# A residual quantizer on one core: the order of all instructions planned by forward and backward passes in place of one pass by due times

## The chip, the cores and the metric

The kernel runs on one core of a Trainium2 chip. The metric is the time on the device in microseconds. The kernel before has three runs, the median is 826.91 us (818.86 to 829.97).

## The reference

```python
# x: (2, 16000, 512) bf16; dw_enc, dw_dec: (3, 512); codebooks: (4, 8, 512)
z = sum(xp[:, i:i+T, :] * dw_enc[i] for i in range(3))      # depthwise, three taps in time
res = z = silu(z)
q = 0
for s in range(4):                                          # residual quantization
    cb = codebooks[s]
    d2 = |res|^2 - 2 res.cb^T + |cb|^2                      # (B, T, 8)
    sel = cb[d2.argmin(-1)]
    q, res = q + sel, res - sel
y = sum(qp[:, i:i+T, :] * dw_dec[i] for i in range(3))      # three taps again
```

For every one of 32000 time steps the input is filtered, passed through SiLU, and replaced by four code words of eight each; each word is picked for what the words before it left over. The output is a filter over the sums of the words.

## The kernel before, in words

The 32000 rows are spread as 128 partitions of 250 rows ("groups"), and the groups are worked off in 16 chunks of 12, then 14 times 16, then 14 groups (`SIZES`). A chunk passes through these tasks:

- *Load.* One transposing DMA for each group and its two neighbours (L358, queue of SP) brings the channels onto the partitions, into XT (two buffers). The first chunk is loaded plainly and transposed on the PE.
- *Front.* For each of four blocks of 128 channels: three products by a tap (L410, DVE), two sums (L418, DVE), then SiLU as exp (L422, ACT), one added (L426, DVE), log (L430, ACT), exp (L433, ACT) and the product (L438, DVE) into RES.
- *Four stages.* `score`: for five or six groups at a time the PE multiplies RES by itself and by the code words into a bank of psG (L489, L494; two banks); `norm` (L502) and `dots` (L505) read it out on DVE. Six small DVE steps (L522 to L549) make a one-hot code; the PE turns it (L559), ACT copies it (L566). Then the chosen words are taken off RES in eight-row pieces: either the PE picks the words (SEL, L584, two banks of psD) and DVE subtracts (L596), or the PE adds RES and the words (NEW, L601 and L584, psA) and ACT writes the sum back (L607). `ON_DVE` says how many of the four blocks go to DVE.
- *Output.* From the turned one-hot codes of the last stage the PE makes the filtered sums of words (Y, L633, psA), ACT copies them out (L639, three buffers YSB), SP's queue stores them (L643).

The order of the instructions on every engine is made in Python while the kernel is built. `Plan.add` takes a task with its engine, the time that it holds the engine (`hold`), the time until its result is there (`delay`), what it needs, and a due time; `take` and `give` name buffers. `Plan.run` plays the tasks through once, with a clock of its own: whenever an engine is free it takes the ready task with the earliest due time for which a buffer is free, and emits its instructions at once. Due times come from the chunk's place (`org`), the period (56) and the stage. Where the PE has nothing to do and was busy for less than 60% of the last 4 planned microseconds (`WARM`), a matmul that fills time goes in (L313). Loads, stores and the steps of the first chunk's load are planned as engines of their own (SP, OUT, ROWS), though loads and stores share SP's queue. The chip's engines each run their instructions in the order emitted and wait for each other by semaphores; the planned times themselves are not in the program.

Of the kernel before, what the change touches and what calls it, by code (L numbers as in the profile page):

```python
# [2 lines left out]

# [14 lines left out]
GC = 16  # L19
# [11 lines left out]
WARM = 0.6  # L31
# [4 lines left out]
PERIOD, LEAD, STAGE, LATE, SPREAD = 56, 0.4, 0.9, 0.3, 0.3  # L36
FAR = -3.3e38


class Plan:  # L40

    def __init__(self, slots):
        self.slots = dict(slots)
# [4 lines left out]
        self.tasks.append((engine, hold, delay, [n for n in needs if n is not None], due, emit, take, give))  # L50
        return len(self.tasks) - 1

    def run(self):
        tasks = self.tasks
        left = [len(t[3]) for t in tasks]
        after = [[] for _ in tasks]
        for n, t in enumerate(tasks):
            for d in t[3]:
                after[d].append(n)
        engines = list(dict.fromkeys(t[0] for t in tasks))  # L60
        ready = {e: [] for e in engines}
        until = {e: 0.0 for e in engines}
        spans = []
        for n, t in enumerate(tasks):
            if not left[n]:
                heapq.heappush(ready[t[0]], (t[4], n))
        now, events, order = 0.0, [], []
        while len(order) < len(tasks):
            going = True
            while going:  # L70
                going = False
                for e in engines:
                    if until[e] > now + 1e-9:
                        continue
                    passed, pick = [], None
                    while ready[e]:
                        due, n = heapq.heappop(ready[e])
                        if all(self.slots[k] > 0 for k in tasks[n][6]):
                            pick = n
                            break  # L80
                        passed.append((due, n))
                    for p in passed:
                        heapq.heappush(ready[e], p)
                    if pick is None:
                        if e == "PE" and self.idle and self.slots["psG"] > 0:
                            while spans and spans[0][1] < now - 4.0:
                                spans.pop(0)
                            if sum(b - max(a, now - 4.0) for a, b in spans) < 4.0 * WARM and self.idle():
                                until[e] = now + 0.3
                                spans.append((now, until[e]))  # L90
                                heapq.heappush(events, (until[e], -1))
                        continue
                    _, hold, delay, _, _, emit, take, _ = tasks[pick]
                    for k in take:
                        self.slots[k] -= 1
                    order.append(pick)
                    emit()
                    until[e] = now + hold
                    if e == "PE":
                        spans.append((now, until[e]))  # L100
                    heapq.heappush(events, (now + hold, -1))
                    heapq.heappush(events, (now + max(hold, delay), pick))
                    going = True
            if len(order) == len(tasks):
                break
            now = events[0][0]
            while events and events[0][0] <= now + 1e-9:
                _, n = heapq.heappop(events)
                if n < 0:
                    continue  # L110
                for k in tasks[n][7]:
                    self.slots[k] += 1
                for a in after[n]:
                    left[a] -= 1
                    if not left[a]:
                        heapq.heappush(ready[tasks[a][0]], (tasks[a][4], a))


@with_exitstack
def kernel(  # L120
# [227 lines left out]
    def load(st, org):  # L348
        g0, G, GP = st["g0"], st["G"], st["GP"]
        done = []  # L350
        if g0 == 0:
            load_rows(st, org)
            return

        def one(n):
            if n == 0:
                st["XT"] = xpool.tile([P, KT, GC + 2, P], BF16, name="XT")
            nc.sync.dma_start_transpose(out=st["XT"][:, :, n, :], in_=group_rows(g0 + n - 1))  # L358

        def edge(n):  # L360
            st["XE"] = const.tile([P, KT, P], BF16, name="XE")
            nc.sync.dma_start_transpose(out=st["XE"], in_=group_rows(0))

        def shift(n):
            XT, XE = st["XT"], st["XE"]
            nc.gpsimd.tensor_copy(XT[:, :, n, 0:P - 1], XE[:, :, 1:P])
            for b in range(B):
                p = (b + 1) * HB - 1
                nc.gpsimd.memset(XT[:, :, n, p:p + 1], 0.0)
            if GP > G:  # L370
                nc.gpsimd.memset(XT[:, :, G + 2:GP + 2, :], 0.0)

        for n in range(G + 2):
            due = org - 2.2 * PERIOD + 0.01 * n
            inside = 0 <= g0 + n - 1 < S
            t = plan.add("SP", 1.4, 2.2, done[-1:], due, (lambda n=n: one(n)) if inside else (lambda n=n: edge(n)),
                         take=("XT",) if n == 0 else ())
            done.append(t)
            if not inside:
                st["edge"] = plan.add("POOL", 1.0, 1.4, [t], due, lambda n=n: shift(n))  # L380
        st["loaded"] = [done[-1], st.get("edge")]

    def front(st, org):
        n, G, MB = st["n"], st["GP"], st["MB"]
# [18 lines left out]
        def block(i):  # L403
# [44 lines left out]
            hold, delay = dve(0.67), dve(0.67) + 0.1  # L448
            z = plan.add("DVE", hold, delay, st["loaded"], due, lambda: product(0), take=("Z",))
            t = plan.add("DVE", hold, delay, st["loaded"], due, lambda: product(1), take=("T",))  # L450
            z = add_up(1, [z, t])
            t = plan.add("DVE", hold, delay, st["loaded"], due, lambda: product(2), take=("T",), give=("XT",) if i == KT - 1 else ())
            st["taps"].append(t)
            z = add_up(2, [z, t])
            e = plan.add("ACT", act(1.8), act(1.8) + 0.12, [z], due, exp, take=("E",))
# [13 lines left out]
    def stage(st, s, due):  # L469
# [11 lines left out]

        def score(q, m):
            RES = st["RES"]
            if q == 0:
                u["TR"] = small.tile([P, GC], BF16, name="TR")
                u["PR"] = small.tile([P, GC, C], BF16, name="PR")
            PS = pending.pop() if pending else psG.tile([P, 512], F32, name="PS")
            V = u["V", q] = PS[:, 0:m * (hi - lo)].rearrange("p (r c) -> p r c", r=m)
            nc.tensor.matmul(V[:, :, own:own + HT], lhsT=IDENT, rhs=MASK[:, 0:m, :], start=True, stop=False, skip_group_check=True)  # L489
            for r in range(m):  # L490
                for i in range(KT):
                    for h in range(2):
                        half = RES[:, i, 2 * (q + r) + h, :]
                        nc.tensor.matmul(V[h * HT:(h + 1) * HT, r, :], lhsT=half[:, LC:LC + HT], rhs=half[:, lo:hi],  # L494
                                         start=False, stop=(i == KT - 1), skip_group_check=True)
            if s == Nq - 1 and q + m == G:
                free["RES"].append(RES)
            if not scored[2:]:
                scored.append(None)
# [9 lines left out]
        for n in range(banks):  # L509
            m = -(-(G - q) // (banks - n))  # L510
            needs = [st["new"][i, j] for i in range(KT) for j in range(q // MB, (q + m - 1) // MB + 1)]
            needs += scored[0:2] + ([codes[st["n"]]] if st["n"] < 3 else [])
            t = plan.add("PE", 0.05 + 0.25 * m, 0.25 + 0.25 * m, needs, due, lambda q=q, m=m: score(q, m), take=("psG",),
                         give=("RES",) if s == Nq - 1 and q + m == G else ())
            seen.append(t)
            maxima.append(plan.add("DVE", 0.07 + 0.065 * m, 0.2 + 0.065 * m, [t], due, lambda q=q, m=m: norm(q, m)))
            maxima.append(plan.add("DVE", 0.06 + 0.01 * m, 0.2, [maxima[-1]], due, lambda q=q, m=m: dots(q, m), give=("psG",)))
            q += m
# [91 lines left out]
        for j in range(0, J, 2):  # L610
            for i in range(KT):
                if i < on_dve[s]:
                    for k in (j, j + 1):
                        c = plan.add("PE", 0.25 * f, 0.25 * f + 0.2, [t, words], due, lambda i=i, k=k: chosen(i, k), take=("psD",))
                        st["new"][i, k] = plan.add("DVE", 0.1 + 0.53 * f, 0.2 + 0.53 * f, [c] + seen, due,
                                                   lambda i=i, k=k: subtract(i, k), give=("psD",))
                    continue
                c = plan.add("PE", 0.86 * f, 0.86 * f + 0.2, [t, words, st["new"][i, j], st["new"][i, j + 1]], due,
                             lambda i=i, j=j: rest(i, j), take=("psA",))
                st["new"][i, j] = st["new"][i, j + 1] = plan.add("ACT", 0.13 + 0.8 * f, 0.25 + 0.8 * f, [c] + seen, due,  # L620
                                                                 lambda i=i, j=j: keep(i, j), give=("psA",))
# [112 lines left out]
```

## Time and profile before

| | before |
|---|---|
| time of the runs, median (lowest to highest) | 826.91 us (818.86 to 829.97) |
| profiled execution, span (its own time is told by the span alone) | 824.6 us |
| PE, matmul | 653.2 us busy, 79% |
| PE, weight load | 314.0 us, 38% |
| DVE | 752.2 us, 91% |
| ACT | 717.8 us, 87% |
| mean granted clock of the PE | 0.912 |
| DMA | 71.82 MB, mean 87 GB/s |

The span runs from the first to the last instruction of one execution. Busy time is time in which an engine executes; an engine that waits for a semaphore is idle. Two instructions of an engine can overlap, so a step from start to start can be shorter than the duration shown. A release ("<- PE SEL L584") names what ended an idle time.

### The profile page before, as it was taken

Reading aid. Unit: us, or ns where it says so; the run is one execution under the profiler, and the core shown is the slowest. Engines: PE = TensorE matmul, PEld = TensorE weight load, DVE = VectorE, ACT = ScalarE, POOL = GpSimd, SP = SyncE. Lnnn points to the kernel's source line nnn. Section 1 sums busy time; section 2 is a strip of 40 time slices with the busy share of each in tenths; the row PEclk is TensorE's granted clock in tenths of the full one; section 3 lists DMA queues with packets and bytes.
Section 4 is the critical chain, followed back from the end, with each engine's and each line's share of the span. In section 5 each row is a group of like instructions: output and inputs, shape, how many; then the busy total and the mean of one; then the engine's idle time right before and its main releaser. Section 6 shows DMA issues by size and latency. Waiting matters only on the chain.

```text
span 824.6 us, 23407 instructions
## 1 busy us (share of the span) xinstructions
PE 653.2 (79%) x10289; PEld 314.0 (38%) x10289; DVE 752.2 (91%) x1584; ACT 717.8 (87%) x623; POOL 7.4 (1%) x17
## 2 busy tenths in 40 slices
PE   3047697898788879868888788779898888989995
PEld 2023333443343444424444244334434434334442
DVE  5987999999999999999999999998989999988871
ACT  2659788898999999999999999998989999886564
POOL 1100000000000000000000000000000000000000
PEclk9566877798998999999999999998979999989998
DMA  7442422152452635253716353451615301111132
GB/s 172 48 98 61 86 52 59 34 117 39 109 111 53 136 70 99 59 119 72 160 53 148 59 117 72 89 138 42 135 44 110 98 36 70 52 79 52 79 143 114
DMA packets 156207, 71.82 MB, mean 87 GB/s; under 512 B 147401, under 2 KB 147786, under 8 KB 155978
## 3 DMA queue, kind: packets, MB, share of 16 engines
q1 hardware_dynamic: 155152, 69.64, 35.8%
q8 instruction: 80, 1.31, 0.7%
q0 software_dynamic: 672, 0.43, 0.5%
q10 hardware_dynamic: 282, 0.26, 0.1%
q14 instruction: 21, 0.17, 0.1%
HBM read 2.39 MB, written 32.77 MB: 43 GB/s over the span
## 4 chain that ended last, share of the span: by engine, by line
ACT 41%; DVE 31%; PE 22%; issue 3%; DMA 2%; ACTq 0%; DVEq 0%
ACT RES L607 11%; ACT LN L430 8%; ACT YSB L639 7%; ACT E L422 7%; ACT E L433 7%; DVE Z L418 6%; DVE RES L596 6%; PE PS L494 6%; PE NEW L601 5%; DVE TR L502 4%; DVE RES L438 3%; DVE T L410 3%; PE NEW L584 3%; PE Y L633 3%; PE SEL L584 2%
## 5 line engine op out<-in xcount | busy, mean ns | idle before, releaser
L607 ACT ACTIVATE RES<-NEW 128x1024 bf16<-128x1024 f32 (+1 forms) x238 | 234.7, 1037 | 29.2 <-PE NEW L584 24.6
L494 PE MATMUL PS<-RES 128*64 128x80 bf16 (+1 forms) x8064 | 189.3, 208 | 27.4 <-DVE RES L438 26.7
L596 DVE TENSOR_TENSOR RES<-RES,SEL 128x512 bf16<-128x512 bf16 (+1 forms) x292 | 185.7, 674 | 19.6 <-PE SEL L584 19.2
L494 PEld LDWEIGHTS <-RES 128*64 128x64 bf16 x8064 | 165.6, 119 | 75.5 <-issue 36.8
L601 PE MATMUL NEW<-RES,IDENT 128*128 128x512 bf16 (+1 forms) x476 | 154.2, 408 | 30.8 <-ACT RES L607 27.0
L418 DVE TENSOR_TENSOR Z<-Z,T 128x2048 bf16<-128x2048 bf16 (+1 forms) x128 | 153.7, 1200 | 0.0
L639 ACT ACTIVATE YSB<-Y 128x1024 bf16<-128x1024 f32 (+1 forms) x126 | 128.1, 1042 | 17.8 <-PE Y L633 12.0
L422 ACT ACTIVATE E<-Z 128x2048 bf16<-128x2048 bf16 (+1 forms) x64 | 122.6, 1916 | 16.2 <-DVE Z L418 16.2
L430 ACT ACTIVATE LN<-E 128x2048 f32<-128x2048 bf16 (+1 forms) x64 | 122.3, 1913 | 8.0 <-DVE E L426 8.0
L433 ACT ACTIVATE E<-LN 128x2048 bf16<-128x2048 f32 (+1 forms) x64 | 122.8, 1920 | 0.2
L502 DVE TENSOR_REDUCE TR<-PS 128x5 bf16<-128x320 f32 (+1 forms) x188 | 95.5, 510 | 17.9 <-PE PS L494 17.5
L633 PE MATMUL Y<-A,OHT 128*128 128x512 bf16 x249 | 86.4, 390 | 30.5 <-ACT RES L607 17.2
L584 PE MATMUL SEL<-OHT,CBN 32*128 32x512 bf16 (+1 forms) x292 | 84.4, 397 | 27.3 <-ACT OHT L566 15.5
L584 PE MATMUL NEW<-OHT,CBN 32*128 32x512 bf16 (+1 forms) x476 | 97.8, 407 | 0.0
L410 DVE TENSOR_SCALAR T<-XT,WENC 128x2048 bf16<-128x2048 bf16 (+1 forms) x128 | 93.5, 740 | 0.0
L584 PEld LDWEIGHTS <-CBN 32*128 32x128 bf16 x768 | 35.2, 92 | 149.9 <-issue 144.4
L438 DVE TENSOR_TENSOR RES<-Z,E 128x2048 bf16<-128x2048 bf16 (+1 forms) x64 | 76.9, 1202 | 6.6 <-ACT E L433 4.0
L601 PEld LDWEIGHTS <-IDENT 128*128 128x128 bf16 x476 | 33.7, 99 | 106.0 <-issue 103.8
L489 PE MATMUL PS<-MASK,IDENT 128*128 128x320 bf16 (+1 forms) x188 | 62.6, 333 | 10.4 <-DVE PR L505 10.1
L633 PEld LDWEIGHTS <-OHT 128*128 128x128 bf16 x373 | 32.5, 98 | 70.2 <-issue 46.9
L566 ACT ACTIVATE OHT<-ps_oh 128x512 bf16<-128x512 bf16 (+1 forms) x64 | 39.7, 623 | 17.0 <-PE ps_oh L559 16.9
L633 PE MATMUL Y<-B,OHT 128*128 128x512 bf16 x124 | 47.4, 383 | 0.1
(73 smaller groups left out, 370.9 us busy)
## 6 DMA issues: line engine op xcount, KB each, us to landing
out_dram<-YSB SPq DMA_DIRECT2D x61, 512.0 KB, 3.2
XT<-in_x_dram SPq DMA_TRANSPOSE x267, 2.8
RES<-in_x_dram SPq DMA_DIRECT2D x1, 1664.0 KB, 6.9
out_dram<-YSB SPq DMA_DIRECT2D x1, 384.0 KB, 2.3
out_dram<-YSB SPq DMA_DIRECT2D x1, 256.0 KB
A<-in_dw_dec_dram POOLq DMA_DIRECT2D x2, 96.0 KB, 5.3
CB<-in_codebooks_dram ACTq DMA_DIRECT2D x1, 128.0 KB
A<-in_dw_dec_dram POOLq DMA_DIRECT2D x2, 64.0 KB, 4.8
```

The lines of the kernel that those rows point to most:

```text
L418: nc.vector.tensor_tensor(out=z, in0=z, in1=t, op=ALU.add)
L422: nc.scalar.activation(u["E"][:, 0:G, :], u["Z"][:, 0:G, :], ACT.Exp, scale=-1.0)
L430: nc.scalar.activation(u["LN"][:, 0:G, :], u["E"][:, 0:G, :], ACT.Ln)
L433: nc.scalar.activation(u["E"][:, 0:G, :], u["LN"][:, 0:G, :], ACT.Exp, scale=-1.0)
L494: nc.tensor.matmul(V[h * HT:(h + 1) * HT, r, :], lhsT=half[:, LC:LC + HT], rhs=half[:, lo:hi], start=False, stop=(i == KT - 1), skip_group ...
L502: nc.vector.tensor_reduce(out=u["TR"][:, q:q + m], in_=u["V", q][:, :, own:own + HT], axis=AX.X, op=ALU.max)
L584: nc.tensor.matmul(ps, lhsT=CBN[s][rows, i * P:(i + 1) * P], rhs=u["OHT"][rows, 0:MB, :], start=start, stop=True, skip_group_check=True)
L596: nc.vector.tensor_tensor(out=old, in0=old, in1=u["SEL", i, j][:, 0:W].rearrange("p (m t) -> p m t", t=HT), op=ALU.add)
L601: nc.tensor.matmul(NEW[:, h, 0:W], lhsT=IDENT, rhs=tokens(i, j + h, 1), start=True, stop=False, skip_group_check=True)
L607: nc.scalar.activation(old, u["NEW", i, j][:, :, 0:W].rearrange("p h (m t) -> p h m t", t=HT), ACT.Copy)
L633: nc.tensor.matmul(Y[:, h, :], lhsT=lhs(), rhs=rhs, start=(a == 0), stop=(a == len(terms) - 1))
L639: nc.scalar.activation(u["YSB"][:, k:k + n, :], u[k][:, 0:n, :], ACT.Copy)
```

## The change

The change rewrites how `Plan.run` finds the order. The plan is played forward with ranks in place of due times, then backward (from the end, with needs and buffers reversed), ranked by when each task ended in the forward pass, then forward again by the backward times, and so on. There are three rounds, each of which begins with ranks disturbed at random from a fixed seed. The last forward pass gives the order and the planned starts; `emit` then hands out the instructions in that order and puts in the matmuls that fill time by the same rule as before (fewer in number: 51 in place of 100).

```diff
+ROUNDS = [(2428, 1.0, 9), (1053, 1.0, 7), (1916, 0.3, 6)]
...
-    def run(self):
+    def pass_over(self, rank, backward=False):
+
         tasks = self.tasks
-        left = [len(t[3]) for t in tasks]
+        needs = [t[3] for t in tasks]
...
+        if backward:
+            needs, after = after, needs
+        takes, gives = (7, 6) if backward else (6, 7)
...
-                        due, n = heapq.heappop(ready[e])
-                        if all(self.slots[k] > 0 for k in tasks[n][6]):
+                        at, n = heapq.heappop(ready[e])
+                        if all(slots[k] > 0 for k in tasks[n][takes]):
...
+    def run(self):
+
+        tasks = self.tasks
+        last = [max(t[1], t[2]) for t in tasks]
+        rank = [t[4] for t in tasks]
+        for seed, spread, passes in ROUNDS:
+            rng = random.Random(seed)
+            starts, order = self.pass_over([r + rng.gauss(0.0, spread) for r in rank])
+            for _ in range(passes):
+                ends, _ = self.pass_over([-(a + d) for a, d in zip(starts, last)], backward=True)
+                starts, order = self.pass_over([-(a + d) for a, d in zip(ends, last)])
+            rank = starts
+        self.emit(starts, order)
```

Beside that, planned times are corrected, and what the order may do is loosened or pinned down in a few places:

```diff
+        room = plan.add("SP", 0.0, 0.0, [], org - 2.2 * PERIOD, place, take=("XT",))
         for n in range(G + 2):
...
-            t = plan.add("SP", 1.4, 2.2, done[-1:], due, (lambda n=n: one(n)) if inside else (lambda n=n: edge(n)),
-                         take=("XT",) if n == 0 else ())
+            t = plan.add("SP", 1.31, 2.9, [room], due, (lambda n=n: one(n)) if inside else (lambda n=n: edge(n)))
...
-        st["loaded"] = [done[-1], st.get("edge")]
+        st["loaded"] = done + [st.get("edge")]
...
-            t = plan.add("DVE", hold, delay, st["loaded"], due, lambda: product(2), take=("T",), give=("XT",) if i == KT - 1 else ())
+            t = plan.add("DVE", hold, delay, st["loaded"] + (st["taps"] if i == KT - 1 else []), due, lambda: product(2), take=("T",), give=("XT",) if i == KT - 1 else ())
...
-            if q == 0:
+            if "TR" not in u:
...
+            if s == Nq - 1 and q + m == G:
+                needs += seen
...
-            t = plan.add("PE", 0.05 + 0.25 * m, 0.25 + 0.25 * m, needs, due, lambda q=q, m=m: score(q, m), take=("psG",),
+            t = plan.add("PE", 0.05 + 0.21 * m, 0.25 + 0.21 * m, needs, due, lambda q=q, m=m: score(q, m), take=("psG",),
...
-                        c = plan.add("PE", 0.25 * f, 0.25 * f + 0.2, [t, words], due, lambda i=i, k=k: chosen(i, k), take=("psD",))
+                        c = plan.add("PE", 0.3 * f, 0.3 * f + 0.2, [t, words], due, lambda i=i, k=k: chosen(i, k), take=("psD",))
...
-                c = plan.add("PE", 0.86 * f, 0.86 * f + 0.2, [t, words, st["new"][i, j], st["new"][i, j + 1]], due,
+                c = plan.add("PE", 0.92 * f, 0.92 * f + 0.2, [t, words, st["new"][i, j], st["new"][i, j + 1]], due,
```

The transposes of a chunk no longer wait for each other in the plan, only for room in XT. The instructions themselves, their sizes and the split between the engines are as before.

More of the change, by code (lines that the diff above doesn't have):

```diff
@@ L2 @@
 import heapq
+import random
 from contextlib import ExitStack
@@ L51, in add @@
         return len(self.tasks) - 1
-    def run(self):
+    def pass_over(self, rank, backward=False):
         tasks = self.tasks
-        left = [len(t[3]) for t in tasks]
+        needs = [t[3] for t in tasks]
         after = [[] for _ in tasks]
-        for n, t in enumerate(tasks):
-            for d in t[3]:
+        for n, ds in enumerate(needs):
+            for d in ds:
                 after[d].append(n)
+        if backward:
+            needs, after = after, needs
+        takes, gives = (7, 6) if backward else (6, 7)
+        left = [len(d) for d in needs]
         engines = list(dict.fromkeys(t[0] for t in tasks))
@@ L62, in run @@
         until = {e: 0.0 for e in engines}
-        spans = []
+        slots = dict(self.slots)
         for n, t in enumerate(tasks):
             if not left[n]:
-                heapq.heappush(ready[t[0]], (t[4], n))
-        now, events, order = 0.0, [], []
-        while len(order) < len(tasks):
+                heapq.heappush(ready[t[0]], (rank[n], n))
+        now, events, order, starts = 0.0, [], [], [0.0] * len(tasks)
+        while True:
             going = True
@@ L76, in run @@
                     while ready[e]:
-                        due, n = heapq.heappop(ready[e])
-                        if all(self.slots[k] > 0 for k in tasks[n][6]):
+                        at, n = heapq.heappop(ready[e])
+                        if all(slots[k] > 0 for k in tasks[n][takes]):
                             pick = n
                             break
-                        passed.append((due, n))
+                        passed.append((at, n))
                     for p in passed:
@@ L84, in run @@
                     if pick is None:
[L85 to L91, printed above, removed]
                         continue
-                    _, hold, delay, _, _, emit, take, _ = tasks[pick]
-                    for k in take:
-                        self.slots[k] -= 1
+                    t = tasks[pick]
+                    for k in t[takes]:
+                        slots[k] -= 1
                     order.append(pick)
[L97 to L102, printed above, removed]
+                    starts[pick] = now
+                    until[e] = now + t[1]
+                    heapq.heappush(events, (now + t[1], -1))
+                    heapq.heappush(events, (now + max(t[1], t[2]), pick))
                     going = True
             if len(order) == len(tasks):
-                break
+                return starts, order
             now = events[0][0]
@@ L110, in run @@
                     continue
-                for k in tasks[n][7]:
-                    self.slots[k] += 1
+                for k in tasks[n][gives]:
+                    slots[k] += 1
                 for a in after[n]:
@@ L115, in run, with emit @@
                     if not left[a]:
-                        heapq.heappush(ready[tasks[a][0]], (tasks[a][4], a))
+                        heapq.heappush(ready[tasks[a][0]], (rank[a], a))
+    def run(self):
[10 more added lines that the diff above has]
+        self.emit(starts, order)
+    def emit(self, starts, order):
+        tasks = self.tasks
+        free, back, spans, end = self.slots["psG"], [], [], 0.0
+        for n in order:
+            engine, hold, delay, _, _, emit, take, give = tasks[n]
+            at = starts[n]
+            if engine == "PE":
+                while end + 0.3 <= at:
+                    while back and back[0] <= end:
+                        free += 1
+                        heapq.heappop(back)
+                    while spans and spans[0][1] < end - 4.0:
+                        spans.pop(0)
+                    if free > 0 and sum(b - max(a, end - 4.0) for a, b in spans) < 4.0 * WARM and self.idle():
+                        spans.append((end, end + 0.3))
+                        end += 0.3
+                    else:
+                        end += 0.1
+                while back and back[0] <= at:
+                    free += 1
+                    heapq.heappop(back)
+                end = at + hold
+                spans.append((at, end))
+            free -= take.count("psG")
+            for _ in range(give.count("psG")):
+                heapq.heappush(back, at + max(hold, delay))
+            emit()
 @with_exitstack
@@ L353, in load, with place @@
             return
+        def place():
+            st["XT"] = xpool.tile([P, KT, GC + 2, P], BF16, name="XT")
         def one(n):
-            if n == 0:
-                st["XT"] = xpool.tile([P, KT, GC + 2, P], BF16, name="XT")
             nc.sync.dma_start_transpose(out=st["XT"][:, :, n, :], in_=group_rows(g0 + n - 1))
@@ L450, in block @@
             t = plan.add("DVE", hold, delay, st["loaded"], due, lambda: product(1), take=("T",))
+            st["taps"] += [z, t]
             z = add_up(1, [z, t])
-            t = plan.add("DVE", hold, delay, st["loaded"], due, lambda: product(2), take=("T",), give=("XT",) if i == KT - 1 else ())
+            t = plan.add("DVE", hold, delay, st["loaded"] + (st["taps"] if i == KT - 1 else []), due, lambda: product(2), take=("T",), give=("XT",) if i == KT - 1 else ())
             st["taps"].append(t)
```

## The prediction

> **What bounds the kernel now.** I read the page's first part, then the busy time by stretches, then VectorE's waits, and last the order of time around single waits.
>
> ```profile
> span 824.6 us, 23407 instructions
> PE 653.2 (79%) x10289; PEld 314.0 (38%) x10289; DVE 752.2 (91%) x1584; ACT 717.8 (87%) x623; POOL 7.4 (1%) x17
> DVE 5987999999999999999999999998989999988871
> ```
>
> VectorE (DVE) is busy for 752.2 of 824.6 us, ScalarE (ACT) for 717.8. Its work is the same after the change, so a new order can only touch the 72.4 us in which VectorE is idle. The next view says where they lie; its columns after the stretch are its length and the busy time of PE, PEld, DVE, ACT and POOL, then the granted clock.
>
> ```profile
> 0.00:13.00 13.00, 1.26 (x15) 1.06 (x16) 3.92 (x24) 1.28 (x1) 0.69 (x6) 1.00 0.87 212
> 13.00:40.00 27.00, 5.62 (x58) 4.75 (x55) 26.45 (x72) 15.30 (x11) 4.74 (x7) 0.63 0.44 62
> 40.00:250.00 210.00, 162.27 (x2416) 77.83 (x2417) 195.62 (x386) 180.30 (x149) 0.00 (x0) 0.82 0.37 76
> 250.00:550.00 300.00, 247.39 (x4184) 121.58 (x4183) 294.68 (x604) 294.36 (x255) 0.00 (x0) 0.98 0.44 95
> 550.00:740.00 190.00, 162.86 (x2509) 74.94 (x2509) 176.62 (x365) 178.40 (x157) 2.01 (x4) 0.92 0.27 76
> 740.00:810.00 70.00, 65.75 (x1081) 30.72 (x1080) 54.86 (x138) 40.27 (x44) 0.00 (x0) 0.99 0.23 91
> 810.00:824.60 14.60, 8.03 (x32) 3.12 (x30) 0.00 (x0) 7.92 (x9) 0.00 (x0) 0.85 0.36 144
> ```
>
> Length minus DVE busy: 9.1 and 0.6 us in the head, 14.4, 5.3 and 13.4 us in the middle (33.1 together), 15.1 us in the drain of the last chunks, 14.6 us behind VectorE's last instruction. In the head the first loads are awaited, at the end only decoding and storing is left; neither depends much on the order. The middle is where an order can win. What ends the idle time there:
>
> ```profile
> DVE RES L596 <- PE SEL L584: 19.2, 30, 2.7
> DVE TR L502 <- PE PS L494: 17.5, 26, 1.9
> DVE RES L438 <- ACT E L433: 4.0, 4, 2.4
> DVE RES L438 <- PE PS L494: 2.6, 5, 1.0
> DVE E L426 <- ACT E L422: 1.2, 2, 0.9
> ```
>
> The numbers are us in total, times, longest. Almost all idle time ends with a matmul that came late: a picked code word that VectorE is to subtract (SEL), or a score that it is to reduce (TR). Of these the drain holds a part, and the calm stretch from 250 to 550 us hardly any (the first two rows below are of 740 to 824.6 us, the last two of 250 to 550 us):
>
> ```profile
> DVE TR L502 <- PE PS L494: 6.4, 10, 1.1
> DVE RES L596 <- PE SEL L584: 5.7, 10, 2.7
> ...
> DVE TR L502 <- PE PS L494: 1.3, 3, 0.5
> DVE RES L596 <- PE SEL L584: 1.3, 4, 0.5
> ```
>
> So outside the drain 13.5 us go to SEL and 11.1 us to TR.
>
> **The change part by part.** It only reorders tasks, corrects planned durations and drops the chain between the loads of a chunk. I set the two instruction orders side by side and counted, for each VectorE instruction that hangs on another engine, how much VectorE work stands between it and the VectorE instruction that sets off its chain: its cover. That work is added up from start-to-start steps as these rows of the order of time show them:
>
> ```profile
> 301.33 0.28 DVE L522 TENSOR_TENSOR V<-PR,TR 128x128 bf16<-128x128 bf16 x1
> 301.53 1.22 DVE L438 TENSOR_TENSOR RES<-Z,E 128x2048 bf16<-128x2048 bf16 x1
> 302.66 0.22 DVE L528 TENSOR_TENSOR D<-V,GPOS 128x128 bf16<-128x128 bf16 x1
> ...
> 790.08 0.29 DVE L522 TENSOR_TENSOR V<-PR,TR 128x128 bf16<-128x128 bf16 x1
> 790.41 0.22 DVE L528 TENSOR_TENSOR D<-V,GPOS 128x128 bf16<-128x128 bf16 x1
> ...
> 791.65 0.29 DVE L549 TENSOR_TENSOR OH<-KEY,M 128x128 bf16<-128x128 f32 x1
> 794.67 1.88 DVE L596 TENSOR_TENSOR RES<-RES,SEL 128x512 bf16<-128x512 bf16 x3 [2.73 <-PE SEL L584]
> ```
>
> *Code words (SEL).* The last two rows are the round trip with no cover at all: one-hot, transpose on PE, copy on ACT, select on PE, 2.73 us idle. The first subtraction of a stage has under 4 us of cover 9 times before and once after, not counting the last three chunks (13 and 4 times with them). Subtractions that directly follow another one, where the two buffers of psD leave PE one step of room, fall from 150 to 61. With the tight places that rare, I leave 2.5 of the 13.5 us: **gain 11**. Bounds: 0, if PE comes late because of its own queue and not for want of cover, and 13.5.
>
> *Scores (TR).* Here the cover shrinks: reductions less than 5 us of VectorE work behind the subtraction that frees their score rise from 19 to 42 (the last three chunks again left out), those under 3.5 us from 9 to 15, those under 2.7 us fall from 6 to 2. Against that stands a truer plan:
>
> ```profile
> 70.08 0.50 PE L489 MATMUL PS<-MASK,IDENT 128*128 128x384 bf16 x1
> ...
> 72.09 0.50 PE L489 MATMUL PS<-MASK,IDENT 128*128 128x384 bf16 x1
> ...
> 305.73 0.30 PE L489 MATMUL PS<-MASK,IDENT 128*128 128x320 bf16 x1
> 305.96 0.84 PE L494 MATMUL PS<-RES 128*64 128x72 bf16 x40
> 306.74 0.40 PE L559 MATMUL ps_oh<-IDENT,OH 128*128 128x128 bf16 x4
> ```
>
> A score of five groups takes 1.01 us of PE (305.73 to 306.74). The old plan held 1.30 us for it, the new one 1.10; over 188 scores the old one booked some 40 us of PE work that isn't there, so PE ran in an order made for another PE. Yet with the low clock of the first stretch a score of six groups takes 2.01 us (70.08 to 72.09), and the new plan's 1.31 is further from that than the old 1.55. Bounds: a loss of 7 us (covers under 3.5 us in all chunks, those behind the SiLU product too: 31 before and 43 after, at 17.5/31 us each) and a gain of 8 us (the 11.1 us falling to the calm stretch's 1.3 us in 300, over 700 us). I take a **gain of 4**, nearer to the calm stretch, since a free score with its 1.01 us fits under 2.7 us even with another PE task ahead of it.
>
> *SiLU chain.* The smallest cover of the product with the inverse (L438) rises from 0.7 to 3.4 us, its median from 6.7 to 12.6; the first exponential's stays at 1.8. Of the 4.0 and 1.2 us of waits for ACT I take away **3**; bounds 0 and 5.2.
>
> *Dependent neighbours.* In the fence above, V followed by work that doesn't need it takes a step of 0.20 us (301.33 to 301.53), V followed by its own reader 0.33 us (790.08 to 790.41). Such pairs fall from 61 to 29 in the order: 32 x 0.13 = **4 us**; bounds 0 (where the pair waits anyway) and 4.
>
> *Drain and end.* VectorE work behind the last one-hot of stage 1 is 25.1 us after and 25.7 before: the drain keeps its shape. Behind the last one-hot copy stand ten output pairs, before nine; the rows of the nine:
>
> ```profile
> 808.68 0.60 ACT L566 ACTIVATE OHT<-ps_oh 128x512 bf16<-128x512 bf16 x1 [6.22 <-PE ps_oh L559]
> 811.23 1.94 ACT L639 ACTIVATE YSB<-Y 128x1024 bf16<-128x1024 f32 x2 [1.95 <-PE Y L633]
> 818.70 1.94 ACT L639 ACTIVATE YSB<-Y 128x1024 bf16<-128x1024 f32 x2 [0.24 <-ACT YSB L639]
> ```
>
> From 811.23 to 820.64 nine of them take 1.05 us each, so one more is a **loss of 1**; bounds -6 and +6 for drain and end together, some four of the waits of up to 1.9 us above.
>
> *Loads.* No wait of VectorE for a load is among the rows, so they are priced at nothing. The cover is VectorE work between a chunk's last transpose and its first product: at least 1.5 us before, at least 4.9 after, against the time to land:
>
> ```profile
> XT<-in_x_dram SPq DMA_TRANSPOSE x267, 2.8
> ```
>
> If that cover were gone, 15 chunks at 2.8 us would cost 42 us; SP issues stores in the same queue, and a store that waits for its copy holds the transposes behind it, but with 12 us of cover in most chunks that isn't near.
>
> **The sum.** 11 + 4 + 3 + 4 - 1 = 21; 824.6 - 21 = 803.6, **804 us**. A second way: the calm stretch idles for 5.3 of 300 us, 1.8%. The middle's 666.9 us of VectorE work at that rate take 678.9 in place of 700 us, again 21 less. The page gives the span alone for the profiled execution; at 824.6 it lies 2.3 us below the median of the three runs, inside their 818.86 to 829.97, so I add nothing.
>
> **The rivals.**
> *A, a trade:* covers are moved from scores to words and nothing is won net. TR at its worst end, -7 for +4, leaves 10 of the 21: 815 us; with SEL at half as well, 820. For it: the counts under 5 us. Against it: those under 2.7.
> *B, the clock falls and PE paces the drain (slower):* matmuls that only fill PE's idle time drop from 100 to 51. The rows of 20 to 30, 60 to 110 and 260 to 310 us:
>
> ```profile
> 20.00:30.00 10.00, 0.07 (x1) 0.00 (x0) 9.52 (x16) 2.01 (x2) 3.79 (x6) 0.51 0.80 88
> 60.00:110.00 50.00, 38.39 (x443) 16.10 (x442) 44.70 (x80) 41.66 (x35) 0.00 (x0) 0.72 0.34 65
> 260.00:310.00 50.00, 40.98 (x663) 19.87 (x661) 49.77 (x101) 49.87 (x43) 0.00 (x0) 1.00 0.44 96
> ```
>
> An idle PE has a clock of 0.51; one busy for 77% of the time had 0.72, one busy for 82% had 1.00. In the drain PE is busy for 65.75 of 70 us at 0.99. At 0.72 that work takes 90.4 us, 24.7 more, which eats the 21: 828 us; at 0.51 it takes 127.6, and the time is 866. It decides from a clock below 0.75. Against it: fillers are still placed wherever the plan shows PE under 60% in 4 us, and at 94% busy the drain hardly needs them. [...]
> *C, more:* the middle goes to nearly no idle time (33.1 to 8) and the neighbours bring 4: 824.6 - 25 - 4 + 1 = 797; with 6 us from the drain, 791.
>
> **How the numbers follow.** Forecast 0.58 (own range 796 to 811), A 0.16, B 0.16, C 0.10. Low end 786: C with nearly the whole 33.1 us (824.6 - 33 - 6). High end 826: A, and B up to where its clock is about 0.73. Some 0.04 lie below and 0.13 above. A measurement here tells about 2%, 16.5 us, from no change: faster means under 810, slower over 843. Faster: 0.52 of the forecast and C's 0.10, 0.62. Slower: 0.10 of B. Within: 0.28.
>
> **What would show it.** Right: waits for SEL outside the drain at 2 to 4 us, TR there at 5 to 9, DVE idle in the middle near 15 us, DVE busy down by 2 to 3 us, end of DVE some 15 us ahead of the end. Wrong: TR waits above 15 us outside the drain (A); a clock under 0.75 from 740 us on, with PE the last in the chain (B); a wait of VectorE for XT, which no step allows; or a middle that idles as before though SEL's cover has grown, which would mean that PE's queue and not cover set those waits.

## The result, and the profile after

The changed kernel takes 818.09 us (median of 20 runs, 809.65 to 824.02), the kernel before 827.28 us in as many (818.86 to 834.35). The ratio is 0.988, 95% interval 0.985 to 0.990: faster by 1.2%, where 2.5% was forecast. 804 was too low; the time lies inside the range of 786 to 826, close to rival A. The profiled execution's span is 814.2 us against 824.6, 10.4 us less.

The page's first lines and the stretches of the changed kernel (columns as before the change; VectorE now ends at 800 us):

```profile
PE 657.9 (81%) x10171; PEld 314.3 (39%) x10240; DVE 750.0 (92%) x1584; ACT 716.7 (88%) x623; POOL 6.9 (1%) x17
```

```profile
0.00:13.00 13.00, 2.56 (x29) 2.54 (x30) 5.35 (x35) 1.28 (x1) 1.06 (x7) 1.00 0.88 212
13.00:40.00 27.00, 4.56 (x44) 3.50 (x41) 26.95 (x64) 13.91 (x10) 4.16 (x7) 0.58 0.49 80
40.00:250.00 210.00, 165.32 (x2459) 78.59 (x2467) 203.72 (x397) 193.16 (x161) 0.00 (x0) 0.81 0.36 79
250.00:550.00 300.00, 258.27 (x4098) 124.15 (x4130) 286.32 (x590) 287.11 (x250) 0.00 (x0) 0.91 0.43 95
550.00:740.00 190.00, 163.31 (x2603) 76.34 (x2622) 180.21 (x381) 175.52 (x154) 1.65 (x4) 0.92 0.28 72
740.00:800.00 60.00, 57.17 (x925) 26.62 (x931) 47.23 (x120) 36.81 (x40) 0.00 (x0) 1.00 0.22 88
800.00:814.20 14.20, 6.68 (x28) 2.52 (x27) 0.24 (x2) 8.91 (x10) 0.00 (x0) 0.95 0.48 194
```

VectorE idles for 6.3 us from 40 to 250 us (14.4 before) and for 9.8 from 550 to 740 (13.4), but from 250 to 550 us, the stretch that had been calm, for 13.7 in place of 5.3. There the granted clock fell from 0.98 to 0.91. The head gives 2 us (5.35 us of work already within 13 us, 3.92 before), drain and end 3. VectorE's waits outside the drain (40 to 740 us), first before, then after:

```profile
DVE RES L596 <- PE SEL L584: 13.5, 20, 2.5
DVE TR L502 <- PE PS L494: 11.1, 16, 1.9
DVE RES L438 <- ACT E L433: 4.0, 4, 2.4
```

```profile
DVE TR L543 <- PE PS L535: 16.7, 22, 1.7
DVE RES L639 <- PE SEL L627: 9.8, 17, 1.1
DVE RES L478 <- PE PS L535: 1.5, 3, 0.9
DVE RES L478 <- ACT LN L470: 0.6, 1, 0.6
```

The wait for the SiLU chain is nearly gone, that for SEL fell by 3.7 us only, that for TR rose by 5.6. The order of time around one such wait in the changed kernel, PE's instructions first, then VectorE's:

```profile
447.75 0.60 PE L627 MATMUL SEL<-OHT,CBN 32*128 32x512 bf16 x2
449.48 0.59 PE L644 MATMUL NEW<-RES,IDENT 128*128 128x512 bf16 x2 [1.13 <-ACT RES L650]
...
453.48 0.53 PE L530 MATMUL PS<-MASK,IDENT 128*128 128x384 bf16 x1
453.94 1.81 PE L535 MATMUL PS<-RES 128*64 128x80 bf16 x48
455.68 0.61 PE L676 MATMUL Y<-A,OHT 128*128 128x512 bf16 x1
...
458.48 0.31 PE L530 MATMUL PS<-MASK,IDENT 128*128 128x320 bf16 x1
458.72 0.91 PE L535 MATMUL PS<-RES 128*64 128x80 bf16 x40
```

```profile
459.67 0.50 DVE L543 TENSOR_REDUCE TR<-PS 128x5 bf16<-128x320 f32 x1 [1.34 <-PE PS L535]
```

PE idles for 1.13 us up to 449.48; two microseconds later PE runs at about half speed: the score from 453.48 takes 2.20 us to the next task, where one of its size took 1.25 nine microseconds earlier. By 458 us the clock is back, but PE is late, and VectorE waits 1.34 us for the score behind. The granted clock says the same (the column of 0.50 and 1.00):

```profile
451.07:457.90 6.83, 6.12 (x62) 3.11 (x62) 6.58 (x16) 5.48 (x6) 0.00 (x0) 0.50 0.19 78
457.90:468.13 10.23, 8.52 (x116) 3.47 (x114) 7.72 (x17) 10.23 (x10) 0.00 (x0) 1.00 0.01 2
```

I call such a time at half clock a spell. By the granted clock that the traces record, 14 spells of together 92 us begin between 60 and 740 us in the kernel before, 22 of 150 us in the changed one. VectorE's waits of over 1 us for PE, from 40 to 740 us, lie within a spell or up to 3 us behind one: 8 of 10 before, 8 of 8 after. So the theory that I tested was: **the clock, not the cover, sets these waits**. By it PE falls to half clock after short idle times (1.13 us ahead of the spell above), the new order has fewer fillers against that, and so the order's gain is spent. The fillers by stretch (250 to 550 us; before, then after):

```profile
250.00:550.00 300.00, 7.34 (x31) 2.75 (x31) 0.98 0.44 95
```

```profile
250.00:550.00 300.00, 2.14 (x8) 0.66 (x8) 0.91 0.43 95
```

The rival is the prediction's A: scores are placed too close behind the subtractions, whatever the clock.

### The profile page after: what moved, and what is told of

It is laid out like the page before. It is cut to its first block, busy times and chain, and to the rows that moved or that the text cites. A ratio compares the mean times of both kernels' runs of the same rounds, so it can differ in the third digit from the quotient of the medians.

```text
span 814.2 us, 23239 instructions
## 1 busy us (share of the span) xinstructions
PE 657.9 (81%) x10171; PEld 314.3 (39%) x10240; DVE 750.0 (92%) x1584; ACT 716.7 (88%) x623; POOL 6.9 (1%) x17
## 3 DMA queue, kind: packets, MB, share of 16 engines
q8 instruction: 80, 1.31, 0.7%
## 5 line engine op out<-in xcount | busy, mean ns | idle before, releaser
L535 PE MATMUL PS<-RES 128*64 128x80 bf16 (+1 forms) x8064 | 193.9, 211 | 34.3 <-DVE RES L478 31.3
L639 DVE TENSOR_TENSOR RES<-RES,SEL 128x512 bf16<-128x512 bf16 (+1 forms) x292 | 193.4, 677 | 13.1 <-PE SEL L627 12.7
L535 PEld LDWEIGHTS <-RES 128*64 128x64 bf16 x8064 | 169.7, 121 | 86.1 <-issue 39.5
L644 PE MATMUL NEW<-RES,IDENT 128*128 128x512 bf16 (+1 forms) x476 | 155.9, 412 | 29.0 <-ACT RES L650 23.8
L462 ACT ACTIVATE E<-Z 128x2048 bf16<-128x2048 bf16 (+1 forms) x64 | 122.6, 1916 | 10.1 <-DVE Z L458 10.0
L627 PE MATMUL SEL<-OHT,CBN 32*128 32x512 bf16 (+1 forms) x292 | 101.7, 404 | 15.3 <-DVE RES L639 12.8
L676 PE MATMUL Y<-A,OHT 128*128 128x512 bf16 x219 | 83.0, 406 | 26.6 <-ACT RES L650 12.1
L530 PE MATMUL PS<-MASK,IDENT 128*128 128x320 bf16 (+1 forms) x188 | 64.4, 343 | 11.3 <-DVE PR L546 9.9
L450 DVE TENSOR_SCALAR Z<-XT,WENC 128x2048 bf16<-128x2048 bf16 (+1 forms) x64 | 47.5, 743 | 0.0
```

The costliest lines, as they stand in the source:

```text
L450: nc.vector.tensor_scalar(out=places(u[name]), in0=taps(i, k), scalar1=WENC[:, i, k:k + 1], scalar2=None, op0=ALU.mult)
L462: nc.scalar.activation(u["E"][:, 0:G, :], u["Z"][:, 0:G, :], ACT.Exp, scale=-1.0)
L627: nc.tensor.matmul(ps, lhsT=CBN[s][rows, i * P:(i + 1) * P], rhs=u["OHT"][rows, 0:MB, :], start=start, stop=True, skip_group_check=True)
L639: nc.vector.tensor_tensor(out=old, in0=old, in1=u["SEL", i, j][:, 0:W].rearrange("p (m t) -> p m t", t=HT), op=ALU.add)
L644: nc.tensor.matmul(NEW[:, h, 0:W], lhsT=IDENT, rhs=tokens(i, j + h, 1), start=True, stop=False, skip_group_check=True)
L676: nc.tensor.matmul(Y[:, h, :], lhsT=lhs(), rhs=rhs, start=(a == 0), stop=(a == len(terms) - 1))
```

## The experiments

All ratios are to the kernel before, run beside it on the same chip.

**Fillers alone.** In the changed kernel fillers are put in after the order is fixed, so `WARM` changes their number and nothing else.

```diff
-WARM = 0.6
+WARM = 0.0      # then 0.75, 0.9, 1.1
```

> The changed kernel without any matmul that only fills PE's idle time (0 in place of 51); the order of all other instructions is that of the changed kernel. Clock theory (most of VectorE's waits outside the drain end on matmuls that ran at half clock, and the clock falls after PE has idled; 51 fillers in place of 100 let it fall more often): the granted clock from 250 to 550 us falls from 0.91 to about 0.85, waits for TR and SEL outside the drain rise from 26 to over 32 us, ratio to the kernel before about 1.00. Cover theory (the scores stand too close behind the subtractions in the new order, whatever the clock): ratio stays at 0.985 to 0.990, the same waits.

820.14 us, ratio 0.990 (0.987 to 0.994); clock from 250 to 550 us 0.89, TR and SEL together 27.5 us outside the drain. The clock theory had asked for a larger loss: the 51 fillers of the changed kernel bring little (0.990 without them, 0.988 with them).

> The changed kernel with fillers wherever the plan has PE busy for under 75% of 4 us in place of 60%: 105 of them in place of 51, all else in the same order. Clock theory: clock from 250 to 550 us up to about 0.95, waits for TR and SEL outside the drain down to about 20 us, ratio about 0.981. Cover theory: no change, 0.985 to 0.990.

811.45 us, 0.982 (0.977 to 0.986), as the clock theory had it; TR and SEL 21.1 us. The clock rose elsewhere than expected, though: from 0.81 to 0.85 in the first stretch and from 0.92 to 0.96 in the last, while the middle one stayed at 0.91.

> The changed kernel with fillers wherever the plan has PE busy for under 90% of 4 us: 193 in place of 51, all else in the same order. Clock theory: clock from 250 to 550 us 0.97 or more, waits for TR and SEL outside the drain down to about 14 us, ratio about 0.975, less what the 142 fillers cost where PE has no time for them (0.22 us each, at most some 10 us). Cover theory: no better than the changed kernel, 0.987 to 0.995, since each filler can only delay.

799.15 us, 0.968 (0.964 to 0.972). Clock 0.91, 0.96 and 0.97 in the three stretches; outside the drain SEL and TR are down to 12.1 us from 26.5:

```profile
DVE TR L543 <- PE PS L535: 7.1, 13, 1.3
DVE RES L639 <- PE SEL L627: 5.0, 10, 1.1
```

The cover theory falls: the order is the same, and more than half of the waits are gone.

> The changed kernel with a filler in every planned gap of PE that has room for one (255 in place of 51), all else in the same order. Clock theory: a little below the 0.968 of the rule at 90%, 0.962 to 0.968, clock from 250 to 550 us at 0.97 or more. If fillers begin to cost: 0.970 to 0.975, with PE the later engine at more waits.

791.78 us, 0.960 (0.955 to 0.965), a little better than expected. Its stretches and waits (40 to 740 us):

```profile
40.00:250.00 210.00, 169.05 (x2658) 81.85 (x2666) 209.16 (x409) 198.78 (x167) 0.00 (x0) 0.94 0.37 82
250.00:550.00 300.00, 264.77 (x4321) 128.40 (x4355) 295.41 (x612) 295.56 (x259) 0.00 (x0) 0.98 0.42 94
550.00:740.00 190.00, 168.87 (x2796) 81.14 (x2815) 185.34 (x406) 170.00 (x155) 1.63 (x4) 0.99 0.28 79
```

```profile
DVE RES L639 <- PE SEL L627: 4.3, 11, 1.2
DVE TR L543 <- PE PS L535: 2.4, 6, 1.0
...
DVE RES L478 <- ACT E L473: 0.2, 1, 0.2
```

The middle idles for 0.8 + 4.6 + 4.7 = 10.1 us (29.8 in the changed kernel, 33.1 before). Spells at half clock: 5 of together 27 us.

**The old order with fillers.** To see what the order is worth where the clock is held, the kernel before was planned as before and emitted afterwards, by the changed kernel's `emit`:

```diff
-                    emit()
+                    starts[pick] = now
...
+                self.emit(starts, order)      # fillers at WARM = 0.9, then 1.1
```

> The order of the kernel before, instruction for instruction on VectorE, ScalarE and SyncE, with fillers put in by the changed kernel's rule at 90% (231 in place of 100; the changed kernel with this rule has 193 and ran at 0.968). It says what the new order is worth where the clock is held up. If clock and order add up (the order worth 1.2% at any clock): ratio about 0.980. If low clock ate the order's gain: the old order gains less from the fillers than the new one's 2.0%, ratio 0.985 to 0.995, so that the orders lie 2 to 3% apart. If the clock alone made everything: about 0.968.

820.26 us, 0.990 (0.985 to 0.994); clock 0.86, 0.97 and 0.96. That is 2.2% behind the new order with this rule (0.968), as expected if low clock ate the order's gain, though the clock isn't quite the same (0.91, 0.96 and 0.97 there).

> The order of the kernel before with a filler in every planned gap of PE (307). The changed kernel's order with the same rule (255) ran at 0.960. If the order is worth 2 to 3% where the clock is held up: 0.983 to 0.992 here, with waits for SEL and TR outside the drain still near 20 us. If the old order only lacked fillers: 0.96 to 0.97.

813.98 us, 0.985 (0.978 to 0.992). Stretches and waits (40 to 740 us):

```profile
40.00:250.00 210.00, 168.75 (x2549) 81.65 (x2550) 199.08 (x393) 184.40 (x153) 0.00 (x0) 0.92 0.36 76
250.00:550.00 300.00, 259.22 (x4216) 126.05 (x4215) 294.76 (x606) 295.23 (x256) 0.00 (x0) 0.99 0.45 99
550.00:740.00 190.00, 170.68 (x2742) 80.75 (x2741) 181.90 (x381) 177.12 (x158) 3.47 (x4) 0.98 0.29 73
```

```profile
DVE RES L628 <- PE SEL L616: 10.2, 15, 2.9
DVE TR L534 <- PE PS L526: 4.7, 7, 1.9
DVE RES L470 <- ACT E L465: 4.3, 5, 2.4
```

At nearly the same clock as the run before it (0.92, 0.99, 0.98 against 0.94, 0.98, 0.99) the old order keeps 10.2 us of SEL and 4.3 us of the SiLU chain, where the new one has 4.3 and 0.2. Fillers bring 1.5% to the old order and 2.8% to the new one; with them the orders stand 814.0 to 791.8, 22 us apart (by the ratios 0.985 and 0.960, 21).

**The parts of the new plan.** Old durations in the new passes:

```diff
-            t = plan.add("PE", 0.05 + 0.21 * m, 0.25 + 0.21 * m, needs, due, lambda q=q, m=m: score(q, m), take=("psG",),
+            t = plan.add("PE", 0.05 + 0.25 * m, 0.25 + 0.25 * m, needs, due, lambda q=q, m=m: score(q, m), take=("psG",),
...                                     # also 0.3 -> 0.25, 0.92 -> 0.86, loads 1.31, 2.9 -> 1.4, 2.2
```

> The changed kernel's forward and backward passes with the planned durations of the kernel before (score 0.25 us a group, picked words 0.25, rest 0.86, loads 1.4 and 2.2 us). If the truer durations carry the gain, this falls back to 0.995 to 1.005 of the kernel before; if the passes carry it, 0.985 to 0.990 stays. Cover theory: the longer planned scores push the reductions further behind the subtractions, so waits for TR outside the drain fall from 16.7 to under 12 us and the ratio to about 0.98. Clock theory: TR waits stay where the clock is low, 14 us or more.

822.5 us, 0.996 (0.993 to 0.999); TR 17.6 and SEL 6.4 us outside the drain, clock 0.85, 0.91 and 0.95. With the old durations, longer planned scores among them, the waits for scores didn't get shorter, again against the cover theory, and without the truer durations two thirds of the gain are gone.

> The forward and backward passes with the planned durations of the kernel before, and a filler in every planned gap of PE (219). If the truer durations carry a part of the gain at full clock: 0.968 or more against 0.960. If the longer planned scores help by leaving room: 0.955.

807.64 us, 0.975 (0.969 to 0.982). With the clock at 0.90, 0.97 and 0.98 it still waits 12.8 us for TR outside the drain. So the truer durations carry some 1.5% of the 4.0% where fillers hold the clock as well; a part of that can be the clock, which is a little lower here than with them (0.94, 0.98 and 0.99).

```diff
-ROUNDS = [(2428, 1.0, 9), (1053, 1.0, 7), (1916, 0.3, 6)]
+ROUNDS = [(0, 0.0, 9)]
```

> The changed kernel with one round of nine forward and backward passes and no disturbed ranks in place of three rounds with seeds (57 fillers; 51 in the changed kernel). If the passes carry the order's gain: ratio 0.985 to 0.992. If the seeds picked a lucky order: 1.00 or above.

812.58 us, 0.982 (0.976 to 0.989): the passes alone bring the gain, and the interval touches that of the three rounds (0.985 to 0.990).

> One round of nine passes without disturbed ranks, with a filler in every planned gap of PE (233). If the rounds with seeds bring anything: worse than 0.960, about 0.965. If they bring nothing on the chip: 0.955 to 0.960, since this order was at 0.9825 with few fillers against 0.988.

794.69 us, 0.960 (0.954 to 0.968), the same as with the three rounds. The disturbed ranks bring nothing that these runs show.

**New durations in the old single pass.**

```diff
-            t = plan.add("SP", 1.4, 2.2, done[-1:], ...
+            t = plan.add("SP", 1.31, 2.9, done[-1:], ...
...                                     # and the three PE durations, the other way round than above
```

> The kernel before, planned in one pass by due times as before, with the changed kernel's planned durations (161 fillers against 100, since the planned PE has more idle time). If the truer durations carry a part of the gain beside the passes: 0.990 to 0.995, of which the 61 further fillers explain up to 0.005. If only passes help: 0.995 to 1.005.

855.91 us, 1.036 (1.030 to 1.041), which neither side had expected. The suspect was the chain of loads, which the change drops together with the new 2.9 us; so once more with the PE durations alone:

> The kernel before with the changed kernel's planned durations of PE alone (119 fillers); the loads are planned as before, chained at 2.2 us. The run with the loads at 2.9 us in that chain was at 1.036. If that chain (18 loads at 2.9 us, 52 us of a period of 56) made it slow: 0.99 to 1.005 here and no wait for XT. If truer PE durations make the single pass worse: 1.02 or more, with waits for TR near 28 us outside the drain.

851.31 us, 1.027 (1.019 to 1.036). Waits from 40 to 740 us:

```profile
DVE TR L502 <- PE PS L494: 27.2, 31, 2.5
DVE RES L596 <- PE SEL L584: 19.3, 29, 2.5
DVE RES L438 <- PE PS L494: 5.9, 6, 2.1
```

The loads are not the main cause: without their new time the kernel is still 2.7% slower than before, and the 0.9% between the two runs lies within their intervals. The granted clock is 0.78, 0.86 and 0.87 here, with 22 spells at half clock of together 198 us. Whether the order that the single pass makes of true durations is itself worse, or only leaves PE the wrong idle times, stays open: this order was not run with more fillers.

## Why the prediction was right or wrong

*The size of the order's gain* was right where fillers hold the clock, and only there: 21 us forecast, 22 us between the two orders with a filler in every gap. As the change came, half of it was missing: 3.3 us less idle time in the middle (18 forecast for SEL, TR and SiLU chain), 2.1 less busy time, 1.9 in the head and 3.0 in drain and end. That the total fits at a held clock is in part luck. There the middle idles for 14.2 us less, VectorE is busy for 3.2 less, and 5.1 come from head, drain and end, which had been priced at a loss of 1.

*The step that failed:* the sum leaves the PE's clock as it was. It prices the 13.5 and 11.1 us of waits for SEL and TR by covers, the second way takes the calm stretch's 0.98 clock and its 5.3 us of idle time as what an order can reach, and the smaller number of fillers is weighed only in rival B, for the drain. In the calm stretch itself the clock went to 0.91 and the idle time to 13.7 us. Fillers fell there from 31 to 8; that this alone brought the clock down is not shown, as 25 of them left it at 0.91. In the drain, where B was placed, the clock stayed at 1.00: B had the falling clock, but in the wrong place.

Two of the prediction's signs of being wrong came: TR above 15 us outside the drain, and a middle that idles nearly as before (29.8 us of 33.1) though SEL's cover has grown. The second was to mean that PE's queue sets these waits; what the fillers show is PE's clock: in the same order with a filler in every gap the granted clock is 0.94, 0.98 and 0.99 in place of 0.81, 0.91 and 0.92, and the waits for SEL and TR are 6.7 us in place of 26.5.

*Words (SEL), gain 11:* 3.7 measured (13.5 to 9.8). In the same order with a filler in every gap 4.3 are left, so the rest hung on PE's speed. Order against order, with fillers in both, the gain is 5.9 (10.2 to 4.3): the cover counts, but for half of the forecast.

*Scores (TR), gain 4:* a loss of 5.6, close to rival A's 7, but not by A's mechanism. With the same short covers and a filler in every gap only 2.4 us are left; against the old order with fillers (4.7) that is a gain of 2.3. That the time came out close to A is luck. The remark that the 1.31 us planned for a score of six groups lies further from the 2.01 at low clock than the old 1.55 named the danger, but the longer time is no cure: the run with the old durations, 1.55 among them, was slower than the changed kernel (0.996 against 0.988). The 40 us of PE work "that isn't there" are the old plan against the new one; against the measured 1.01 us a score they would be 54.

*SiLU chain, gain 3:* right and more: 4.0 and 1.2 us became 0.6, and the wait of L438 for PE fell from 2.6 to 1.5.

*Neighbours, 4:* half. VectorE's busy time fell by 2.1 us (752.15 to 750.03), inside the 2 to 3 that the signs gave for it; that it was these pairs was not tested alone.

*Drain and end, a loss of 1:* a gain of some 3 (15.1 to 12.8, 14.6 to 14.0); the tenth pair cost nothing that shows. *Head, 0:* 2 gained, not foreseen: the steps that make the mask (1.3 us) now stand ahead of the wait for the code book. *Loads, 0:* right, no wait of VectorE for XT in the changed kernel.

## What to carry to other kernels

When an order is changed, look at what it does to the clock of the PE before its covers are counted: here the new order ran with 22 spells at half clock of together 150 us in place of 14 of 92, and half of its gain was missing. The filler rule of the old order went with a clock of 0.98 from 250 to 550 us there and of 0.91 in the new one. Tune fillers again after each change of order; here a filler in every planned gap took the changed kernel from 818.1 to 791.8 us; no version was faster. And compare two orders at a held clock, or the clock is what one compares.

## What the runs showed of the hardware that was not expected

PE fell to half clock though it was never idle for long. In the traces before and after the recorded clock is 1.0 or 0.5, and a spell that begins between 60 and 740 us lasts one to four times 3.41 us (13.65 us the longest). I counted by windows of 3.41 us. In the changed kernel, behind the first 100 us, the longest idle time of PE in the two windows ahead of a spell was 2.0 us, and in the last one PE was busy for 40 to 71%, so 1.0 to 2.0 us of idle time in a window went ahead of these falls.

Idle time alone doesn't tell them: from 250 to 550 us PE was busy for under 70% in 16 windows of the kernel before and in 15 of the changed one, but there were 2 falls against 9. Nor does the recorded clock always follow an idle PE: from 13 to 40 us PE was busy for 4.6 of 27 us in the changed kernel, at a clock of 0.58, and for 5.0 us in the run without fillers, at 1.00. What PE streams in a window separates the falls better in these two traces. I weighed each matmul by its columns and by its shape against the largest, 128*128 (SEL, 32*128, a quarter; a score, 128*64, half; a filler, 128*128, one), as a share of what matmuls of the largest shape stream in a window at full clock (512 columns in 0.215 us, the step of the Y matmuls at full clock). Of the windows at full clock from 60 to 740 us 37 had a share below 0.37, and 35 of these were followed by half clock; of the other 285 none was. From 250 to 550 us the kernel before has 2 windows below 0.37, the changed one 9, as many as falls. The 0.37 was set on the same two traces that it sorts, so it is a count on these two; no run was made to test it.

The number of fillers alone doesn't tell the clock either: with 25 of them from 250 to 550 us in the run at 75% it was 0.91 there, with 31 in the kernel before 0.98. What the old order would do without its fillers was not run.
